# A sparse-attention and mixture-of-experts kernel on one core: keys blocked from PSUM, block sums moved to GpSimd, the last batch in two parts

## The chip, the cores and the metric

The program runs on 1 core of a Trainium2 chip. A core has TensorE (PE in the profile, its weight loads PEld), VectorE (DVE), ScalarE (ACT), GpSimd (POOL) and SyncE (SP, which here only issues DMAs). The metric is the device time of one execution in microseconds.

## The reference

Four batches, eight heads, 768 positions, 64 numbers a head. Each query sees the keys less than 16 positions away, and 24 block keys (the elementwise maximum of 32 keys each) with 24 block values (the mean of 32 values). The result goes through four experts' causal attention; each token uses its best two.

```python
k_sum = k.reshape(B, H, nb, block, D).max(axis=3)     # block = 32, nb = 24
v_sum = v.reshape(B, H, nb, block, D).mean(axis=3)
scores_l = scale * np.matmul(q, k.transpose(0, 1, 3, 2))
mask_l = np.abs(pos[:, None] - pos[None, :]) < window   # window = 16
scores_s = scale * np.einsum('bhsd,bhnd->bhsn', q, k_sum) + np.log(block)
a = softmax(np.concatenate([np.where(mask_l, scores_l, -1e9), scores_s], axis=-1))
x = np.matmul(a, np.concatenate([v, v_sum], axis=2))   # heads side by side: (B, S, 512)
logits = x @ w_gate                                     # best 2 of 4 experts, softmax weights w
for e in range(E):
    q, k, v = x @ wq[e], x @ wk[e], x @ wv[e]
    ye = causal_softmax(scale * (q @ k.transpose(0, 2, 1))) @ v @ wo[e]
    out += (expert e is chosen) * w * ye
```

## The kernel before

The work of each batch has two stages. **Stage 1** goes by pairs of heads (four pairs `c` a batch). The keys and queries of a pair come as 96 rows of 8 positions (`dk`, `dq`, DMAs that GpSimd issues) and are turned on TensorE (`tk`, `tq`: 16 matmuls of 96 columns). The turned keys go from PSUM to a tile `kT` (`ck`), and from there into `kw` (`kw`): 12 overlapping windows of 96 positions for 12 blocks of 64 queries. The block keys come from three halving maxima on VectorE (`km`), two more turned matmuls (L324), a short maximum (`rk`) and a copy of them behind each of the 12 windows (`ksc`). Queries are copied and reordered (`cq`). Then `sc` (mask plus scores, two halves), `ex` (exponentials on ScalarE), `av` (24 matmuls a half, L408), `rc` and `xm` (division), `tx` (turning, L433) and `hi`, `lo` (the result as two 16-bit parts).

The values come straight into `vb` (`dv`): 96 rows for each of 24 windows, so that every window's edge rows are loaded twice. Rows 96 to 119 hold the block sums: `bs` multiplies the windows by a 0-1 matrix `sel` on TensorE (L294), `be` takes them out of PSUM, `ds` copies them to the 12 windows of a head.

**Stage 2** goes by batch: `vp` (values and gate logits), `lg`, `v2`, `ga`, `gx`, `gb`, `gc` (gates); for each of two pairs of experts `pp` (projections, L582), `pc`, six score units `sp` (L606) with exponentials `es` (L614) and GpSimd's causal cut `dm` (L619); `aw` (three pieces, L630); `r2`, `wv` (division and gate), `tw`, `ct` (turning), and for both pairs `op`, `oc`, `od` (output projection, copy, store).

The order is written out by hand: `TABLE` lists each step's number, engine (P, V, A, G, S) and buffer slots, and `emit` issues them so. Each engine runs its own steps in that order, and a step that waits holds up all behind it on its engine. Step names end in batch and pair: `tk12` is pair 2 of batch 1.

## Time and profile before

| | |
|---|---|
| Median of 3 runs | 196.94 us (196.18 to 202.36) |
| Profiled execution, its own time | 197.88 us |
| Its span, first to last instruction | 196.1 us |
| Busy share PE, DVE, ACT, POOL | 83%, 71%, 58%, 41% |
| PE instructions | 3568 matmuls, 3568 weight loads |

Busy shares are means over the span; matmuls are pipelined and their ends are modelled, so PE's share is higher than what its steps need. The chain that ended last names, at each moment, what the end was waiting for; "issue" there is time in which an engine waited for nothing that the profile shows.

### The profile page before, as it was taken

What the parts mean: (1) busy time and instruction counts of PE and PEld (TensorE: products, weight loads), DVE (VectorE), ACT (ScalarE), POOL (GpSimd) and SP (SyncE); (2) the same over time, 40 slices, a digit from 0 to 9 for tenths busy, and PEclk for the clock granted to TensorE, in tenths of its full rate; (3) what the DMA queues carried; (4) which work ended last, traced back from release to release, by engine and by line L of the source; (5) the groups of instructions that cost most, each with busy time, mean ns of one, the idle gap of its engine ahead of it and who ended that gap; (6) DMA issues with size and microseconds to landing.
All of it is one profiled execution on the core that took longest, in us unless ns stands there. A gap on an engine that the chain in (4) does not pass through costs nothing.

```text
span 196.1 us, 7990 instructions
## 1 busy us (share of the span) xinstructions
PE 162.3 (83%) x3568; PEld 127.2 (65%) x3568; DVE 140.0 (71%) x279; ACT 113.1 (58%) x152; POOL 80.3 (41%) x137
## 2 busy tenths in 40 slices
...
GB/s 70 202 208 187 202 173 147 206 192 165 176 228 195 163 76 142 110 199 163 73 3 142 297 190 41 79 3 110 3 214 7 0 5 3 0 3 77 241 128 201
DMA packets 53986, 24.63 MB, mean 126 GB/s; under 512 B 44480, under 2 KB 50624, under 8 KB 53952
## 3 DMA queue, kind: packets, MB, share of 16 engines
...
q14 instruction: 6, 0.05, 0.1%
...
## 4 chain that ended last, share of the span: by engine, by line
PE 66%; DVE 19%; issue 7%; ACT 3%; DMA 3%; DVEq 0%; ACTq 0%; POOLq 0%
PE ps L408 13%; PE ps L582 8%; PE ps L294 7%; PE ps L630 6%; PE ps L433 5%; DVE kw L167 5%; PE ps L671 5%; PE ps L517 4%; PE ps L606 4%; PE ps L384 4%; DVE km L251 3%; PE ps L321 3%; PE ps L391 3%; DMA kn<-in_k_dram 3%; PE ps L362 2%
## 5 line engine op out<-in xcount | busy, mean ns | idle before, releaser
L614 ACT ACTIVATE a<-ps 128x1024 f16<-128x1024 f32 (+1 forms) x48 | 41.9, 918 | 6.5 <-PE ps L606 5.9
L619 POOL TENSOR_SCALAR_AFFINE_SELECT a<-a 128x256 f16<-128x256 f16 x48 | 19.6, 426 | 52.5 <-ACT a L614 52.0
L398 ACT ACTIVATE aT<-ps 120x768 f32<-120x768 f32 x32 | 25.3, 812 | 20.9 <-PE ps L391 18.8
L167 POOL COPY kw<-kT 128x960 f16<-128x960 f16 (+1 forms) x20 | 24.5, 1256 | 25.6 <-ACT kT L165 23.4
L408 PE MATMUL ps<-vb,aT 120*64 120x65 f32 x768 | 28.3, 230 | 5.0 <-issue 3.8
L408 PEld LDWEIGHTS ps<-vb,aT 120*64 120x64 f32 x768 | 25.5, 143 | 7.8 <-issue 5.6
L582 PE MATMUL ps<-hi,wqk 128*128 128x384 f16 x128 | 22.5, 326 | 0.0
L294 PE MATMUL ps<-vb,sel 96*32 96x64 f32 x768 | 18.4, 233 | 4.7 <-issue 4.7
L294 PEld LDWEIGHTS ps<-vb,sel 96*32 96x32 f32 x768 | 16.2, 118 | 6.6 <-issue 6.2
L167 POOL COPY vb<-vs 24x1536 f32<-24x1536 f32 x8 | 12.9, 1611 | 14.5 <-DVE vs L167 12.2
L582 PEld LDWEIGHTS <-wqk 128*128 128x128 f16 x128 | 12.0, 98 | 8.2 <-issue 0.5
L321 PE MATMUL ps<-id,kn 96*64 96x96 f16 x256 | 9.9, 230 | 8.6 <-DMA kn<-in_k_dram 6.6
L423 DVE TENSOR_TENSOR x<-ps,rec 128x768 f32<-128x768 f32 x16 | 15.3, 958 | 0.6
L444 DVE TENSOR_TENSOR lo<-ps,hi 128x768 f16<-128x768 f32 x16 | 14.9, 954 | 0.9 <-ACT hi L165 0.5
L606 PE MATMUL ps<-qk,qk 64*128 64x512 f16 (+3 forms) x128 | 14.7, 307 | 0.7 <-DVE ob L167 0.4
L165 ACT COPY kT<-ps 128x768 f16<-128x768 f16 x8 | 6.4, 801 | 15.2 <-PE ps L324 11.8
L384 PE MATMUL ps<-pi,mt 64*128 64x64 f16 (+1 forms) x128 | 12.7, 271 | 2.8 <-DVE pi L202 1.4
L321 PEld LDWEIGHTS <-kn 96*64 96x64 f16 x256 | 8.3, 128 | 9.8 <-DMA kn<-in_k_dram 6.6
L517 PE MATMUL ps<-wvg,hi 128*128 128x264 f16 x96 | 13.8, 275 | 0.0
L433 PE MATMUL ps<-id,x 128*128 128x128 f32 x96 | 13.3, 278 | 0.1
L671 PE MATMUL ps<-wo,wT 128*128 128x512 f16 x48 | 12.7, 397 | 0.6 <-ACT a L614 0.3
L391 PE MATMUL ps<-qT,kw 64*128 64x64 f16 x384 | 12.5, 201 | 0.0
...
## 6 DMA issues: line engine op xcount, KB each, us to landing
vb<-in_v_dram SPq DMA_DIRECT2D x14, 576.0 KB, 10.2
...
```

The source lines that it names most:

```text
L167: en(e).tensor_copy(dst, src)
L294: nc.tensor.matmul(pbank(sp)[32 * j:32 * j + 32, 0, 0:64], T["sel"][:, 22 - 2 * tt:54 - 2 * tt], T["vb"][vb[b, cs[j // 2]].slot][0:WIN, 12 ...
L321: nc.tensor.transpose(pbank16(kp)[64 * hp:64 * hp + 64, 96 * s:96 * s + 96], src[:, hh + hp, 64 * s:64 * s + 64], T["id16"][0:96, 0:96])
L384: nc.tensor.matmul(s[:, hp, 64 * t0:64 * t1], T["mt"][r, var, :], T["pi"][r, t0:t1, :], start=(i == 0), stop=False, skip_group_check=True)
L398: nc.scalar.activation(T["aT"][aT.slot][0:KR], pbank(sc, 2)[0:KR, :, 0:384], AF.Exp, scale=SCALE)
L408: nc.tensor.matmul(pbank(av, 2)[o:o + 64, u, 65 * (2 * (t // 2) + hp):65 * (2 * (t // 2) + hp) + 65], a[0:KR, hp, 64 * t:64 * t + 64], T[" ...
L433: nc.tensor.transpose(pbank(xp, 2)[:, t // 3, 128 * (t % 3):128 * (t % 3) + 128], T["x32"][x32.slot][:, 128 * t:128 * t + 128], T["id32"])
L517: nc.tensor.matmul(p[:, i, 0:264], hi_(ch)[:, cols], T["wvg"][:, ch, :], start=(ch == 0), stop=False, skip_group_check=True)
L582: nc.tensor.matmul(pbank(pp, 2)[:, u, 0:384], T["wqk"][:, cc, ch, j, :], hi_(ch)[:, 384 * u:384 * u + 384], start=(ch == 0), stop=(ch == N ...
L606: nc.tensor.matmul(pbank(sp, 2)[:, ep, c0:c0 + w], T["qk"][qk[1].slot][r, 128 * tj:128 * tj + 128], T["qk"][qk[0].slot][r, n0:n0 + w], sta ...
L614: nc.scalar.activation(a2v(u), pbank(sp, 2)[:, :, 0:ln], AF.Exp, scale=SCALE / (XS * XS))
L671: nc.tensor.matmul(pbank(op, 2)[:, i, :], T["wT"][wTs[cc].slot][:, 128 * ti:128 * ti + 128], T["wo"][:, cc, :], start=(cc == 0), stop=(cc ...
```

## The change

1. `kw` and `rk` read the turned keys in PSUM themselves. `ck`, `kT`, `km` and the turned maxima are gone; `rk` takes the maximum over all 32 keys. The keys start at PSUM column 2, and two small matmuls fill two columns on either side, so that one copy makes all 12 windows.
2. `dv` loads 64 rows of a window and one column more; `hc` copies the other 32 rows on chip.
3. Block sums stay on TensorE for batch 0 and the first half of batch 1, with both heads of a pair in one matmul of 128 columns. For five groups of four heads (`TREE`), `dvs` loads the values once more, 32 positions a row, and `tr` adds halves on GpSimd; `ds` copies from the result.
4. In the last batch `r2` to `od` run for tiles 0 to 3 and 4 to 5 apart; the last store is two of one tile.
5. 46 matmuls on a tile of zeros stand in front (`f` in the table).
6. `TABLE` is written anew.

```diff
+PE0 = 2
+TREE = {(1, 1), (2, 0), (2, 1), (3, 0), (3, 1)}
...
-SLOTS = dict(qn=3, kn=3, km=3, kT=2, ks=3, kw=3, qT=3, aT=6, x32=2, vb=6, vs=2,
-             rec=2, hi=8, lo=8, v2=2, lgp=2, gt=2, qk=3, a2=2, cmb=2, wav=2,
+SLOTS = dict(qn=3, kn=3, ks=3, kw=3, qT=3, aT=6, x32=2, vb=6, vs=2, vt=1, vu=2,
+             rec=3, hi=8, lo=8, v2=2, lgp=2, gt=2, qk=3, a2=2, cmb=2, wav=2,
...
-116,S,0 27,G,0 28,G,0 29,V,0 30,V, 31,V, 10,G, 76,P,0.0.0 12,V, 5,G,1 77,A, 94,P,1.1.1 99,P,2.0 78,V, 80,V,0
+f,P,7.46 104,S, 2,G,0 0,G, 3,G,0 6,V, 4,G, 53,P,0.0.0 55,V, 36,P,1.1.1 37,A, 56,A, 1,G, 40,P,2.0 38,V, 41,A,
...
-            for w in (256, 128, 64):
-                def mx(e, w=w, i=i):
-                    hs = slice(n * i, n * i + n)
-                    m = T["km"][km[b, g].slot][:, hs, :]
-                    x = T["kn"][kn[b, g].slot][:, hs, :] if w == 256 else m
-                    en(e).tensor_tensor(m[:, :, 0:w], x[:, :, 0:w], x[:, :, w:2 * w], AL.max)
-                ne = w * n
-                R.step(f"km{b}{g}{i}_{w}", {"V": 0.07 + ne * 0.00053},
-                       [kn[b, g]] if w == 256 else [km[b, g]], [km[b, g]], mx)
...
-                          [[D, WIN], [64 * D, t1 - t0], [1, D]])
-            nc.sync.dma_start(out=w[0:WIN, t0:t1, 0:64], in_=src)
-        if edge:
-            R.step(f"zv{b}{c}", {"V": 0.1, "G": 0.14}, [vones], [vb[b, c]], zv)
-        R.step(f"dv{b}{c}", {"S": 0.9 if edge else 0.45}, [vones, vb[b, c]] if edge else [vones],
...
+            src = bass.AP(vh.tensor, vh.offset + (64 * i0 - 16) * D,
+                          [[D, 64], [64 * D, 24 - i0], [1, D]])
+            nc.sync.dma_start(out=w[0:64, i0:24, 0:64], in_=src)
+            t0 = 64 * 24 - 16
+            if last:
+                for h in (0, 16):
+                    nc.sync.dma_start(out=w[h:h + 16, 24:25, 0:64], in_=rows(t0, 16))
+            else:
+                nc.sync.dma_start(out=w[0:32, 24:25, 0:64], in_=rows(t0, 32))
+        R.step(f"dv{b}{c}", {"S": 1.35 if first or last else 0.9}, [], [vb[b, c], vr[b, c]], dv,
+               dma=(64 * 24 + 32) * 0.0215 / 16)
+
+        def edge(e):
+            w = T["vb"][vb[b, c].slot]
+            copy(e, w[64:96, 0:24, 0:64], w[0:32, 1:25, 0:64])
+        R.step(f"hc{b}{c}", {"G": 1.65, "A": 1.45, "V": 0.9}, [vr[b, c]], [vb[b, c]], edge)
...
+        npair = len(cs)
+        ways = 4 // npair
 
         def mm(e):
-            n = 2 * len(cs)
-            for tt in range(NQ):
-                for j in range(n):
-                    nc.tensor.matmul(pbank(sp)[32 * j:32 * j + 32, 0, 0:64],
-                                     T["sel"][:, 22 - 2 * tt:54 - 2 * tt],
-                                     T["vb"][vb[b, cs[j // 2]].slot][0:WIN, 12 * (j % 2) + tt, 0:64],
-                                     start=(tt == 0), stop=(tt == NQ - 1))
-        R.step(f"bs{b}{cs[0]}", {"P": 1.35}, [vb[b, c] for c in cs] + [sel], [sp], mm,
-               mode=3, keep=[t])
+            for tt in range(NQ + 1):
+                for i in range(npair):
+                    j = ways * i + tt % ways
+                    nc.tensor.matmul(
+                        pbank(sp)[32 * j:32 * j + 32, 0, 0:128].rearrange("p (h d) -> p h d", h=2),
+                        T["sel"][:, 24 - 2 * tt:56 - 2 * tt],
+                        T["vb"][vb[b, cs[i]].slot][0:64, tt:tt + 13:12, 0:64],
+                        start=(tt < ways), stop=(tt + ways > NQ))
+        R.step(f"bs{b}{cs[0]}", {"P": 0.03 + 0.054 * npair * 13 * 4 / 4},
...
+            for i in range(npair):
+                dst = T["vs"][t.slot][96:120, i, :]
+                for w in range(ways):
+                    j = ways * i + w
+                    src = pbank(sp)[32 * j:32 * j + NSUM, 0, 0:128]
+                    if w == 0:
+                        copy(e, dst, src)
+                    else:
+                        nc.vector.tensor_tensor(dst, src, dst, AL.add)
+        opts = {"V": 0.25 * 4}
...
             def dsum(e, i=i, c=c):
-                copy(e, T["vb"][vb[b, c].slot][WIN:KR, :, 0:64].rearrange("n (h t) d -> n h t d", h=2),
-                     T["vs"][t.slot][WIN:KR, 2 * i:2 * i + 2, :].unsqueeze(2).to_broadcast(
-                         (NSUM, 2, NQ, 64)))
-            R.step(f"ds{b}{c}", {"G": 1.65, "V": 0.87, "A": 1.4}, [t, vones], [vb[b, c]], dsum)
+                copy(e, T["vb"][vb[b, c].slot][WIN:KR, 0:24, 0:64].rearrange("n (h t) d -> n h t d", h=2),
+                     T["vs"][t.slot][WIN:KR, i, :].rearrange("n (h d) -> n h d", h=2).unsqueeze(
+                         2).to_broadcast((NSUM, 2, NQ, 64)))
+            R.step(f"ds{b}{c}", {"G": 1.55, "V": 0.96, "A": 1.45}, [t], [vb[b, c]], dsum)
...
+    def tree(b, g):
+        t, u = R.buf("vt"), R.buf("vu")
+
+        def load(e):
+            for j in range(4):
+                nc.sync.dma_start(out=T["vt"][t.slot][32 * j:32 * j + NSUM, :],
+                                  in_=v[b, 4 * g + j].rearrange("(n s) d -> n (s d)", s=32))
+        R.step(f"dvs{b}{g}", {"S": 1.8}, [vtz], [t], load, dma=3.0)
+        for i, ws in enumerate(((1024,), (512, 256, 128, 64))):
+            def add(e, ws=ws):
+                x = T["vt"][t.slot]
+                for w in ws:
+                    y = T["vu"][u.slot] if w == 64 else x[:, 0:w]
+                    en(e).tensor_tensor(y[0:120], x[0:120, 0:w], x[0:120, w:2 * w], AL.add)
+            R.step(f"tr{b}{g}{i}", {"G": sum(0.13 + w * 0.00218 for w in ws)}, [t],
+                   [u] if i else [t], add, keep=[t])
+        for c in (2 * g, 2 * g + 1):
+            def dsum(e, c=c):
+                for h in range(2):
+                    j = 32 * (2 * (c % 2) + h)
+                    copy(e, T["vb"][vb[b, c].slot][WIN:KR, 12 * h:12 * h + 12, 0:64],
+                         T["vu"][u.slot][j:j + NSUM, :].unsqueeze(1).to_broadcast((NSUM, NQ, 64)))
+            R.step(f"ds{b}{c}", {"G": 1.75, "V": 0.95, "A": 1.64}, [u], [vb[b, c]], dsum)
...
-        kp, kT, ks, kw = R.buf("ps"), R.buf("kT"), R.buf("ks"), R.buf("kw")
+        kp, ks, kw = R.buf("ps"), R.buf("ks"), R.buf("kw")
+
+        def turn(dst, src):
+            for s in range(8):
+                for hp in range(2):
+                    c0 = PE0 + 96 * s
+                    nc.tensor.transpose(dst[64 * hp:64 * hp + 64, c0:c0 + 96],
+                                        src[:, hh + hp, 64 * s:64 * s + 64], T["id16"][0:96, 0:96])
...
         def tk(e):
             src = T["kn"][kn[b, g].slot]
-            for s in range(8):
-                for hp in range(2):
-                    nc.tensor.transpose(pbank16(kp)[64 * hp:64 * hp + 64, 96 * s:96 * s + 96],
-                                        src[:, hh + hp, 64 * s:64 * s + 64], T["id16"][0:96, 0:96])
+            turn(pbank16(kp), src)
             for hp in range(2):
-                nc.tensor.transpose(pbank16(kp)[64 * hp:64 * hp + 64, 768:864],
-                                    T["km"][km[b, g].slot][:, hh + hp, 0:64], T["id16"][0:96, 0:96])
-        R.step(f"tk{b}{c}", {"P": 0.37}, [kn[b, g], km[b, g], id16], [kp], tk, mode=2, keep=[kT, ks])
-
-        def ck(e):
-            copy(e, T["kT"][kT.slot], pbank16(kp)[:, 0:S])
-        R.step(f"ck{b}{c}", {"V": 0.56, "A": 0.80}, [kp], [kT], ck)
...
+                x = pbank16(kp)[64 * hp:64 * hp + 64, :]
+                nc.tensor.transpose(view(x, 0, [[PE0 + 768, 2], [1, 2]]),
+                                    src[0:4, hh + hp, 0:64], T["id16"][0:4, 0:4])
+        R.step(f"tk{b}{c}", {"P": 0.38}, [kn[b, g], id16], [kp], tk, mode=2, keep=[kw, ks])
+
+        def kwc(e):
+            copy(e, T["kw"][kw.slot][:, :, 0:WIN].rearrange("c t (p s) -> c t p s", s=8),
+                 view(pbank16(kp), 0, [[8, NQ], [1, 12], [96, 8]]))
+        R.step(f"kw{b}{c}", {"V": 1.32, "A": 1.13}, [kp, kwpad], [kw], kwc)
 
...
         def rk(e):
             nc.vector.tensor_reduce(T["ks"][ks.slot],
-                                    pbank16(kp)[:, 768:864].rearrange("c (n p) -> c n p", p=4),
-                                    AX.X, AL.max)
-        R.step(f"rk{b}{c}", {"V": 0.20}, [kp], [ks], rk)
-
-        def kwc(e):
-            w = T["kw"][kw.slot]
-            t = T["kT"][kT.slot]
-
-            def src(off, n, step, m):
-                return bass.AP(t.tensor, t.offset + off,
-                               [list(t.ap[0]), [step, n], [1, m], [96, 8]])
-            copy(e, w[:, 1:NQ - 1, 0:WIN].rearrange("c t (p s) -> c t p s", s=8), src(6, 10, 8, 12))
-            dst = bass.AP(w.tensor, w.offset + 16,
-                          [list(w.ap[0]), [11 * 128 - 16, 2], [8, 10], [1, 8]])
-            copy(e, dst, src(0, 2, 86, 10))
-        R.step(f"kw{b}{c}", {"G": 2.24, "V": 1.20}, [kT, kwpad], [kw], kwc)
+                                    view(pbank16(kp), PE0, [[4, NSUM], [96, 8], [1, 4]]),
+                                    AX.XY, AL.max)
+        R.step(f"rk{b}{c}", {"V": 0.92}, [kp], [ks], rk)
...
+        cuts = [(0, 6)] if b < B - 1 else [(0, 4), (4, 6)]
...
+            for h, (i0, i1) in enumerate(cuts):
...
+                def r2(e, cc=cc, avv=avv, cm=cm, i0=i0, i1=i1):
...
+        outs = [(0, 2), (2, 4), (4, 6)] if b < B - 1 else [(0, 2), (2, 4), (4, 5), (5, 6)]
...
+            R.step(f"op{b}{t2}", {"P": 0.4325 * n}, [wd[0][h], wd[1][h], wo], [op], ops,
+                   keep=[ob] + wTs)
...
     def fill(bank, n):
+        nc.vector.memset(T["zz"], 0.0)
         for _ in range(n):
-            nc.tensor.matmul(T["ps"][:, bank, 0:128], T["id16"], T["id16"], start=True, stop=True)
+            nc.tensor.matmul(T["ps"][:, bank, 0:128], T["zz"], T["zz"], start=True, stop=True)
...
-            if b:
+            if (b, g) in TREE:
+                tree(b, g)
+            elif b:
                 sums(b, [2 * g, 2 * g + 1])
...
-    many("vb", (128, 24, 65), FP32)
-    many("vs", (128, 4, 64), FP32)
+    many("vb", (128, 25, 65), FP32)
+    many("vs", (128, 2, 128), FP32)
+    many("vt", (128, 2048), FP32)
+    many("vu", (128, 64), FP32)
```

What each engine now does, at three places. ScalarE at its start; `kT` are turned keys, `kw` the windows, `ks` block keys, `qT` queries, `aT` exponentials. Before:

```order
L165 ACT_TABLE_LOAD
L165 COPY kT_82<-ps 128x768
L165 COPY qT_91<-ps 128x768
L165 COPY qT_90<-ps 128x768
L398 ACTIVATE aT_94<-ps 120x768
L398 ACTIVATE aT_93<-ps 120x768
L165 COPY qT_92<-ps 128x768
L165 COPY kT_83<-ps 128x768
```

Now:

```order
L166 ACT_TABLE_LOAD
L166 COPY kw_84<-ps 128x12x96
L166 COPY kw_83<-ks_80 128x12x24
L166 COPY qT_86<-ps 128x768
L166 COPY kw_83<-ps 128x12x96
L166 COPY qT_87<-ps 128x768
L429 ACTIVATE aT_89<-ps 120x768
L429 ACTIVATE aT_90<-ps 120x768
```

The copy of turned keys to `kT` is gone, and ScalarE makes the windows itself out of PSUM.

GpSimd in the expert stage of batch 0; `a` are the exponentials that it cuts, `vb` value tiles, `vt` and `vu` the tree's rows. Before:

```order
L167 COPY kw_87<-kT_82 128x10x96
L167 COPY kw_87<-kT_82 128x2x80
L619 AFFINE_SELECT a_136<-a_136 128x2x128 x2
L619 AFFINE_SELECT a_136<-a_136 128x256
L619 AFFINE_SELECT a_136<-a_136 128x2x128 x2
L241 DMA qn_73<-in_q_dram 96x4x512
L167 COPY vb_106<-vs_107 24x24x64
L619 AFFINE_SELECT a_136<-a_136 128x2x128 x3
L619 AFFINE_SELECT a_136<-a_136 128x256
L241 DMA kn_80<-in_k_dram 96x4x512
L619 AFFINE_SELECT a_136<-a_136 128x2x128 x2
```

Now:

```order
L340 TENSOR_TENSOR vt_105<-vt_105 120x1024
L653 AFFINE_SELECT a_136<-a_136 128x2x128
L340 TENSOR_TENSOR vt_105<-vt_105 120x512
L340 TENSOR_TENSOR vt_105<-vt_105 120x256
L340 TENSOR_TENSOR vt_105<-vt_105 120x128
L340 TENSOR_TENSOR vu_107<-vt_105 120x64
L653 AFFINE_SELECT a_136<-a_136 128x256
L653 AFFINE_SELECT a_136<-a_136 128x2x128 x4
L168 COPY vb_100<-vu_107 24x12x64 x2
L168 COPY vb_99<-vb_99 32x24x64
L653 AFFINE_SELECT a_137<-a_137 128x256
```

The windows `kw` have left this queue; the additions of a tree stand between the cuts.

VectorE at the end of the program; `cmb` and `wav` are factors and weighted values, `wT` the turned ones, `ob` output tiles. Before:

```order
L642 RECIPROCAL cmb_138<-ps 128x12
L644 TENSOR_TENSOR cmb_138<-cmb_138,gt_132 128x12
L648 TENSOR_TENSOR wav_140<-ps,cmb_138 128x2x6x64
L642 RECIPROCAL cmb_139<-ps 128x12
L644 TENSOR_TENSOR cmb_139<-cmb_139,gt_132 128x12
L648 TENSOR_TENSOR wav_141<-ps,cmb_139 128x2x6x64
L167 COPY wT_144<-ps 128x768
L167 COPY wT_145<-ps 128x768
L167 COPY ob_146<-ps 128x1024
L167 COPY ob_148<-ps 128x1024
```

Now:

```order
L683 RECIPROCAL cmb_138<-ps 128x2x4
L685 TENSOR_TENSOR cmb_138<-cmb_138,gt_132 128x2x4
L690 TENSOR_TENSOR wav_140<-ps,cmb_138 128x2x4x64
L683 RECIPROCAL cmb_139<-ps 128x2x4
L685 TENSOR_TENSOR cmb_139<-cmb_139,gt_132 128x2x4
L690 TENSOR_TENSOR wav_141<-ps,cmb_139 128x2x4x64
L683 RECIPROCAL cmb_139<-ps 128x2x2
L685 TENSOR_TENSOR cmb_139<-cmb_139,gt_132 128x2x2
L690 TENSOR_TENSOR wav_141<-ps,cmb_139 128x2x2x64
L168 COPY wT_145<-ps 128x256
L168 COPY wT_145<-ps 128x512
L168 COPY ob_148<-ps 128x1024
```

The division of the last expert pair ends with a piece of 2 tiles in place of 6, and one output copy is left here in place of two.

## Rows read from the trace of the kernel before

**Rows 1.** Four stretches: length, busy PE, PEld, DVE, ACT, POOL, PE clock, DMA.

```profile
6.60:43.30 36.70, 30.77 (x804) 27.63 (x805) 28.46 (x60) 19.02 (x30) 18.54 (x32) 1.00 1.19 189
43.30:81.40 38.10, 35.32 (x774) 27.66 (x775) 31.59 (x63) 25.55 (x34) 15.46 (x24) 0.96 1.07 165
81.40:141.00 59.60, 49.65 (x1216) 39.05 (x1215) 44.32 (x85) 34.09 (x47) 30.08 (x36) 0.94 0.60 107
141.00:191.00 50.00, 46.59 (x778) 32.89 (x776) 35.62 (x73) 33.15 (x44) 11.46 (x25) 1.00 0.18 65
```

**Rows 2.** The chain that ended last, shares of the span by engine.

```profile
PE 66%; DVE 19%; issue 7%; ACT 3%; DMA 3%; DVEq 0%; ACTq 0%; POOLq 0%
```

**Rows 3.** The chain in order of time: start, length, what; front and block sums.

```profile
1.36 5.24 DMA kn<-in_k_dram
...
16.26 0.64 PE ps L321 x16
...
31.12 1.50 PE ps L294 x48
...
67.69 1.49 PE ps L294 x96
```

**Rows 4.** The chain: a long copy, and a wait inside block sums.

```profile
52.04 4.35 DVE kw L167 x2
...
111.90 1.15 PE ps L294 x70
113.05 4.31 issue
117.36 1.01 PE ps L294 x26
```

**Rows 5.** The chain: TensorE steps at full clock.

```profile
38.60 1.42 PE ps L408 x48
...
50.86 0.34 PE ps L321 x16
...
86.62 0.47 PE ps L517 x4
...
138.25 1.31 PE ps L433 x12
...
152.16 2.60 PE ps L582 x16
```

**Rows 6.** Instructions grouped by line and shape: count, busy us, mean ns, idle before.

```profile
L614 ACT ACTIVATE a<-ps 128x1024 f16<-128x1024 f32 x40 | 39.4, 1025 | 3.8 <-PE ps L606 3.4
...
L398 ACT ACTIVATE aT<-ps 120x768 f32<-120x768 f32 x32 | 25.3, 812 | 20.9 <-PE ps L391 18.8 <-DVE vs L167 1.9
...
L165 ACT COPY qT<-ps 128x768 f16<-128x768 f16 x11 | 8.7, 804 | 6.5 <-PE ps L362 6.5
...
L167 DVE COPY qT<-ps 128x768 f16<-128x768 f16 x5 | 4.7, 948 | 0.5 <-PE ps L362 0.5
```

**Rows 7.** The same view, two copies on GpSimd.

```profile
L167 POOL COPY kw<-kT 128x960 f16<-128x960 f16 x10 | 19.4, 1942 | 25.6 <-ACT kT L165 23.4 <-DVE kT L167 2.2
...
L167 POOL COPY vb<-vs 24x1536 f32<-24x1536 f32 x8 | 12.9, 1611 | 14.5 <-DVE vs L167 12.2 <-PE ps L391 2.1
```

**Rows 8.** Instructions in order of time: block-key copies on VectorE, a GpSimd copy.

```profile
12.70 2.48 POOL L167 COPY kw<-kT 128x960 f16<-128x960 f16 x2 [0.84 <-DVE kT L167]
...
13.01 1.85 DVE L167 COPY kw<-ks 128x288 f16<-128x288 f16 x1
...
19.74 0.24 DVE L167 COPY kw<-ks 128x288 f16<-128x288 f16 x1
```

**Rows 9.** DMA issues: count, KB each, median us from issue to landing.

```profile
vb<-in_v_dram SPq DMA_DIRECT2D x14, 576.0 KB, 10.2
```

**Rows 10.** The chain: the end of the program.

```profile
182.82 1.29 PE ps L630 x42
...
189.78 1.23 DVE ob L167
```

297 lines of the change are left out of this document (151 added, 146 removed).

## The prediction

> **What bounds the kernel now.** I read the chain of waits first, then busy time by stretch, then single steps. The chain is 66% TensorE, 19% VectorE and 7% issue [rows 2]: TensorE sets the pace, but much of it is waiting. I cut the run where the projections (`pp`) of batches 0, 1 and 2 begin: 6.6 to 43.3 us (stage A), to 81.4 (B), to 141.0 (C), and to the last engine instruction at 191.0 (D). In these 36.7, 38.1, 59.6 and 50.0 us [rows 1] PE shows 31 to 50 us busy, but a matmul's row holds its latency too, so I count PE by steps, from back-to-back rows at full clock [rows 5]: a projection step `pp` (8 matmuls of 384 columns) 1.30 us, 0.423 ns a column; by that rate a score step `sc` 0.33 to 0.35, the 12 `sp` of a batch 2.3 to 2.4, an output step `op` 0.87; a value step `vp` 2 x 0.47 and small matmuls, 1.1; `av` 0.71; `tx` 0.66; a turn `tk` or `tq` 0.34; `aw` 0.43 a piece, from 1.29 for three [rows 10]; `tw` 0.34. A block-sum step is 1.5 either way, 48 matmuls with two side by side or 96 with four [rows 3].
>
> Stage B before: 4 `pp` 5.2, 3 `vp` 3.3, `sp` 2.4, 5 turns 1.8, 2 `bs` 3.0, 4 `sc` 1.4, 8 `av` 5.7, 4 `tx` 2.6, 6 `aw` 2.6, 2 `tw` 0.7, 2 `op` 1.7: 30.3 us. The same count gives 41.6 for C and 42.6 for D. So PE works 30.3 of 38.1 (0.79), 41.6 of 59.6 (0.70), 42.6 of 50.0 (0.85). In A, VectorE is the fullest, 28.46 of 36.7 (0.776) [rows 1]. The rest is waits between engines. Three kinds are plain. TensorE runs at half clock in the front: 16 turns take 0.64 us there and 0.34 later [rows 3, 5], 1.2 against 2.4 GHz. VectorE's copies from SBUF to SBUF stand still while GpSimd works: a copy of block keys takes 1.85 us beside a GpSimd copy and 0.24 elsewhere [rows 8], and the windows `kw` once held the chain for 4.35 us [rows 4]. And TensorE stops for 4.31 us inside one block-sum step, after 70 of 96 matmuls and with no step's wait in between [rows 4]: it seems to have had no instructions.
>
> **The change, part by part.** *Block sums.* 768 matmuls (10 steps, 15.0 us) become 156 of 128 columns: twice the columns, so 2 x 1.49/96 = 31 ns each, 4.8 us. TensorE saves 10.2 us. Nothing else fills that time on PE.
>
> *Instructions of PE.* 3568 matmuls become 3568 - 612 + 46 = 3002, 16% fewer, and the block sums, which use up instructions fastest (16 ns a matmul), are mostly gone. I count the 4.31 us stop as gone and leave the other issue pieces. The Trainium skill, "Runtime: NRT & Kernel Launch", Instruction fetch mechanics, says that fetching is mostly hidden, since instructions issue more slowly than they are loaded; by that the stop has another cause and stays, and stage C below would be 3.5 us longer. The row inside the step speaks against it.
>
> *Keys.* `ck`, `km` and GpSimd's `kw` leave. `kw` now reads 1152 elements in PSUM: ScalarE takes 0.80 us for 768 and 1.03 for 1024 [rows 6], so 1.13; below 0.80 is excluded, and above I allow 1.4. Queries are read with the same step today, at 0.80. `rk` reads 768 in place of 96 elements, 0.95 as VectorE's query copy [rows 6]. So VectorE loses its long SBUF work and gains 16 x 0.7 us in PSUM.
>
> *Values.* `hc` copies 32 rows of 1536 elements, which is GpSimd's 1.6 us of `ds` [rows 7]; 13 run there. A tree adds 1984 elements: between 1.05 ns (that copy) and 2.0 ns an element (the strided `kw` copy, 1942 ns for 960) [rows 7], 2.1 to 4.0 us; two inputs make me take 4.0. In C GpSimd then has 3 trees 12, 15 `dm` 6.2, `hc` and `ds` 11, DMA issues and the rest 4: 33 us, a little below the others.
>
> *Front.* The zeros run within the 5.2 us that the first keys take [rows 3]; 46 at 57 to 114 ns (128 columns, full or half clock) need 2.6 to 5.2 us and cost nothing; without that cover they would cost up to that. They may leave the clock at full; A is bound elsewhere, so I credit nothing. Value loads no longer wait for GpSimd's clearing and now run beside the first keys: 0 to 2 us later keys, 0.5 taken.
>
> *End.* Before: last `aw` ends at 184.1, last copy at 191.0 [rows 10], 6.9 us. Now two small VectorE operations 0.4, a third of `wv` 0.4, 2 turns 0.2, copy 0.3, six output tiles 2.6 and a copy of one tile 0.6, with hand-overs some 5.3: 1.6 saved. The last store is half as large: 5.1 us behind the last copy become 4.6.
>
> **The sum.** Work of the fullest engine in each stage of the new order, over the share that was reached there. A: ScalarE, 7 `kw` 7.9, 8 `cq` 6.4, 11 `ex` 8.9, 3 `hi` 2.4, 3 `ksc` 1.3, `ds` 1.5: 28.4 (VectorE 27.9, PE 20.9); over 0.776, 36.6. B: PE 25.0 (30.3 less 3 `aw`, two turns, one `bs`, one `tw`, two `op`, and one `sc` more), VectorE 24.6, ScalarE 24.0; over 0.79, 31.6. C: PE 36.0, VectorE 36.2, ScalarE 35.4; the share without the stop is 41.6 of 55.3, 0.75, so 48.0. D: PE 44.9 (more of batch 3's `av` and `tx` fall here), ScalarE 39.9, VectorE 38.6; over 0.85, 52.8, less the end's 1.6. With 7.1 in front and 4.6 behind: 7.1 + 36.6 + 31.6 + 48.0 + 51.2 + 4.6 = 179.1. The profiled execution was 197.88 us with a span of 196.1, so 1.8 lie around it; the median is 0.9 lower. **Forecast: 180 us.** With 0.85 in every stage the four are 134.3/0.85 = 158.0, and the time 169; with 0.74, 181.5, and the time 192.
>
> **Rivals.** *(a) Three full engines.* ScalarE goes from 112 [rows 1] to 129 us, VectorE from 140 to some 128, PE falls to 127. If what PE gives back is eaten by waits for these two, only the block sums' 10.2 us go: 187. For it: the shares above were reached with one full engine; against it: part of VectorE's 140 were waits for GpSimd.
>
> *(b) VectorE stands still beside GpSimd.* GpSimd goes from 80 to some 100 us, and 13 SBUF copies remain on VectorE (`ksc` 5, `ds` 6, `hc` 2). If each is stretched by the 1.6 us of [rows 8], VectorE has 21 us more, some 17 of it on the path: 197 us, no change. Against it: 26 such copies (`kw`, `ksc`, `ds`) and 27 `km` stood there before. The Trainium skill, "SBUF — State Buffer", Who interferes with whom, has the rule: whichever of GpSimd and a VectorE copy in a two-port mode starts first holds the shared port pair for its whole instruction. By that rule PSUM reads are free of it, and the rows agree as far as the block-key copy goes.
>
> *(c) The trees come late; slower.* There is one tile `vt`. A tree's load waits for the last one's additions, and SyncE holds all later value loads and stores behind it, GpSimd all later `dm`, for which `aw` waits. A cycle is a landing, 10.2 us as a value load's [rows 9], and 4 us of adding; four of them fit into the 80 us of B and C. From 20 us a cycle on they don't: at 26, PE waits 6 us four times, 204 us.
>
> *(d) Still faster.* All shares at 0.85 or more, below 169 us.
>
> **How the numbers follow.** Forecast with its spread, 169 to 185: 0.56. (a), 185 to 193: 0.24. (b), 193 to 201: 0.08. (c), above 201: 0.07. (d): 0.05. Two per cent, about what a measurement of this kernel can tell from no change, is 193 to 201. The range 169 to 193 leaves out 0.20. Faster 0.85, same 0.08, slower 0.07.
>
> **What would show it.** The projections of batches 0, 1 and 2 begin near 44, 75 and 123 us; PE shows some 3000 matmuls and L294's successor about 5 us; no issue piece above 2 us; windows from PSUM near 1.13 us on ScalarE; a tree near 4 us; VectorE busy near 128 us. Wrong would be: a wait of `dm` or `ds` for a tree's load, VectorE copies of block keys above 1 us all over, the first keys landing after 9 us, or stage A longer than 37 us because ScalarE's queue, which now holds seven window copies, holds back the exponentials.

## The result and the profile after

The changed kernel takes 187.2 us (median of four runs, 184.9 to 187.9) where the kernel before, run beside it, takes 198.4. The ratio is 0.948, with an interval from 0.932 to 0.965; run once more in E1 it is 0.941 (0.931 to 0.951). The forecast of 180 us named the direction, and its range holds the time, but the gain is 11 us and not 17. Single runs of one kernel lie up to 8 us apart here (183.9 to 192.2 in E1), so small differences are read from the intervals and from stretches of the trace, not from single times. The ratios compare only the fast runs of both kernels, those within some 1.5% of the fastest of their kernel, so a median that holds slower runs can lie higher than its ratio suggests.

The page of the changed kernel (busy time by engine; queue, packets, MB and share; the chain by engine):

```profile
span 186.2 us, 6923 instructions
...
PE 158.9 (85%) x3002; PEld 122.4 (66%) x3002; DVE 131.9 (71%) x254; ACT 120.8 (65%) x155; POOL 100.1 (54%) x150
...
q8 instruction: 23, 0.38, 1.0%
...
PE 48%; DVE 22%; DMA 9%; issue 7%; POOL 6%; ACT 5%; POOLq 0%; DVEq 0%; ACTq 0%
```

TensorE has its 3002 matmuls and GpSimd its 100 us, as worked out; ScalarE has 121 us and not 129, VectorE 132 and not 128. Yet "issue", time in which TensorE waits for nothing that the profile shows, is 7% as before [rows 2]. The queue q8 carries instructions: 0.38 MB in 23 packets are 16 KB each; and 0.44 MB (0.06 more come by another queue) for 6923 instructions are 64 bytes each. So a packet holds 256 instructions, for TensorE 128 weight loads with their matmuls. The kernel before had 28 such packets for 7990 instructions.

The four stretches of the prediction, in the changed kernel (windows; columns as in [rows 1]):

```profile
6.10:45.10 39.00, 31.65 (x770) 27.12 (x770) 27.51 (x65) 23.99 (x30) 18.23 (x28) 0.82 1.24 183
45.10:78.50 33.40, 30.03 (x561) 23.72 (x560) 26.11 (x46) 23.85 (x30) 21.67 (x26) 0.95 0.95 137
78.50:126.90 48.40, 41.85 (x855) 31.69 (x855) 38.62 (x63) 33.48 (x45) 37.90 (x51) 1.00 0.87 157
126.90:181.40 54.50, 50.28 (x777) 35.02 (x774) 39.38 (x79) 38.21 (x51) 17.69 (x32) 1.00 0.28 82
```

| us | before | forecast | after | after less forecast |
|---|---|---|---|---|
| up to the first keys | 6.6 | 7.1 | 6.1 | -1.0 |
| A | 36.7 | 36.6 | 39.0 | +2.4 |
| B | 38.1 | 31.6 | 33.4 | +1.8 |
| C | 59.6 | 48.0 | 48.4 | +0.4 |
| D | 50.0 | 51.2 | 54.5 | +3.3 |
| behind | 5.1 | 4.6 | 4.8 | +0.2 |
| span | 196.1 | 179.1 | 186.2 | +7.1 |

The gain comes from B and C; A is longer than before. The front, in the timeline of TensorE (start, length, line, what, idle time before and its end):

```profile
6.08 0.85 PE L360 MATMUL ps<-id,kn 96*64 96x96 f16 x16
...
7.00 0.56 PE L360 MATMUL ps<-id,kn 96*64 96x96 f16 x16
...
11.13 1.49 PE L360 MATMUL ps<-id,qn 96*64 96x96 f16 x32 [3.45 <-DMA qn<-in_q_dram]
```

The first keys are turned at 6.08 us, half a microsecond earlier than before and not half a microsecond later. The queries are late instead: TensorE stands for 3.45 us, and behind that it works at half rate again (32 turns in 1.49 us; 16 took 0.56 just before, and 32 take 0.87 at 111.38). The costs of single steps (groups: busy, mean ns):

```profile
L340 POOL TENSOR_TENSOR vt<-vt 120x1024 f32<-120x1024 f32 (+3 forms) x20 | 25.0, 1248 | 5.5 <-DMA vt<-in_v_dram 4.3
...
L381 DVE TENSOR_REDUCE ks<-ps 128x24 f16<-128x768 f16 x16 | 14.9, 952 | 10.1 <-PE ps L371 5.9
...
L168 POOL COPY vb<-vb 32x1536 f32<-32x1536 f32 x13 | 18.9, 1461 | 2.8 <-DMA vb<-in_v_dram 2.1
...
L166 ACT COPY kw<-ps 128x1152 f16<-128x1152 f16 x10 | 11.2, 1121 | 12.9 <-PE ps L371 7.2
```

The window copy (1.12 us for 1.13), the maxima (0.95) and the edge copy (1.46 for 1.6) are as priced. The row of the trees holds four of a tree's five additions; with the last, narrow one (1.6 us for all five) a tree is 26.6/5 = 5.3 us, above the bounds of 2.1 to 4.0. The block sums left on TensorE show 7.1 us busy, where about 5 were expected.

Last, the stops, the pieces of the chain called "issue" (start, length, what):

```profile
30.23 1.64 issue
...
56.05 2.09 issue
58.14 0.28 PE ps L640
58.42 4.51 PE ps L439 x96
...
105.59 2.34 POOL vt L340
...
120.12 1.16 issue
```

The stop of 4.31 us inside a block-sum step [rows 4] is gone, but the text had counted on no stop above 2 us, and there is one of 2.09, with 96 matmuls of `av` behind it at 47 ns each, where they take 33 at full rate (72 in 2.41 us at 72.08); the granted clock is 0.50 in the first 2 us of them. At 105.59 the chain runs over GpSimd's tree; E12 shows what that is.

### The profile page after: what moved, and what is told of

Same layout as the page of the kernel before. It is cut to its first block, busy times and chain, and to the rows that moved or that the text cites. A ratio compares the mean times of both kernels' runs of the same rounds, so it can differ in the third digit from the quotient of the medians.

```text
span 186.2 us, 6923 instructions
## 1 busy us (share of the span) xinstructions
PE 158.9 (85%) x3002; PEld 122.4 (66%) x3002; DVE 131.9 (71%) x254; ACT 120.8 (65%) x155; POOL 100.1 (54%) x150
## 4 chain that ended last, share of the span: by engine, by line
PE 48%; DVE 22%; DMA 9%; issue 7%; POOL 6%; ACT 5%; POOLq 0%; DVEq 0%; ACTq 0%
PE ps L439 10%; PE ps L616 7%; DMA vb<-in_v_dram 5%; PE ps L464 5%; PE ps L360 5%; DMA qn<-in_q_dram 4%; PE ps L548 4%; PE ps L718 3%; PE ps L640 3%; POOL vt L340 3%; DVE ks L381 2%; DVE wav L690 2%; PE ps L415 2%; PE ps L297 2%; PE ps L664 2%
## 5 line engine op out<-in xcount | busy, mean ns | idle before, releaser
L653 POOL TENSOR_SCALAR_AFFINE_SELECT a<-a 128x256 f16<-128x256 f16 x48 | 18.6, 406 | 42.1 <-ACT a L648 29.3
L340 POOL TENSOR_TENSOR vt<-vt 120x1024 f32<-120x1024 f32 (+3 forms) x20 | 25.0, 1248 | 5.5 <-DMA vt<-in_v_dram 4.3
L381 DVE TENSOR_REDUCE ks<-ps 128x24 f16<-128x768 f16 x16 | 14.9, 952 | 10.1 <-PE ps L371 5.9
L168 POOL COPY vb<-vb 32x1536 f32<-32x1536 f32 x13 | 18.9, 1461 | 2.8 <-DMA vb<-in_v_dram 2.1
L166 ACT COPY kw<-ps 128x1152 f16<-128x1152 f16 x10 | 11.2, 1121 | 12.9 <-PE ps L371 7.2
L415 PE MATMUL ps<-pi,mt 64*128 64x320 f16 (+1 forms) x128 | 11.8, 259 | 3.5 <-POOL vt L340 2.6
L360 PE MATMUL ps<-id,qn 96*64 96x96 f16 x256 | 9.0, 226 | 4.3 <-DMA qn<-in_q_dram 3.4
L664 PE MATMUL ps<-v,a 128*128 128x65 f16 x336 | 12.0, 193 | 0.6 <-ACT wT L166 0.6
L664 PEld LDWEIGHTS <-a 128*128 128x128 f16 x336 | 11.2, 97 | 2.0 <-issue 1.4
L166 ACT COPY qT<-ps 128x768 f16<-128x768 f16 x11 | 8.6, 805 | 5.9 <-PE ps L360 5.9
```

The costliest lines, as they stand in the source:

```text
L166: nc.scalar.copy(dst, src)
L168: en(e).tensor_copy(dst, src)
L340: en(e).tensor_tensor(y[0:120], x[0:120, 0:w], x[0:120, w:2 * w], AL.add)
L381: nc.vector.tensor_reduce(T["ks"][ks.slot], view(pbank16(kp), PE0, [[4, NSUM], [96, 8], [1, 4]]), AX.XY, AL.max)
L664: nc.tensor.matmul(pbank(av, 2)[:, ep, 65 * ti:65 * ti + 65], a2v(u)[:, ep, o:o + 128], T["v2"][v2.slot][:, tj, 2 * cc + ep, :], start=(tj ...
```

## The experiments

All were run beside the kernel before, and the column of the ratio is against it (for E12 too few runs could be compared). `pp` is where the projections of batches 0, 1 and 2 begin in the profiled run, and D+ the time from the last of these to the end of the span.

| | median (lowest to highest), us | ratio (95% interval) | profiled span | pp 0, 1, 2 | D+ |
|---|---|---|---|---|---|
| after | 187.2 (184.9-187.9) | 0.948 (0.932-0.965) | 186.2 | 45.1, 78.4, 126.8 | 59.5 |
| E1 after again | 186.7 (183.9-192.2) | 0.941 (0.931-0.951) | 185.0 | 47.1, 76.5, 125.6 | 59.5 |
| E2 no zeros | 191.3 (187.8-193.5) | 0.957 (0.948-0.967) | 190.8 | 51.9, 82.3, 130.1 | 60.7 |
| E3 values held | 189.9 (183.8-191.6) | 0.936 (0.924-0.947) | 189.7 | 45.9, 79.8, 130.2 | 59.5 |
| E4 held, zeros | 188.5 (184.4-191.9) | 0.940 (0.930-0.949) | 188.5 | 47.1, 79.1, 127.9 | 60.6 |
| E5 short keys | 191.5 (187.6-192.7) | 0.956 (0.947-0.965) | 190.1 | 49.4, 81.5, 130.6 | 59.5 |
| E6 light trees | 194.9 (193.6-196.7) | 0.990 (0.983-0.996) | 192.4 | 47.2, 82.7, 132.6 | 59.8 |
| E7 sums on TensorE | 234.9 (234.1-236.2) | 1.194 (1.188-1.200) | 232.4 | 45.5, 80.7, 143.4 | 89.0 |
| E8 one tail | 189.8 (184.9-191.9) | 0.944 (0.935-0.954) | 190.2 | 46.8, 80.0, 130.3 | 59.8 |
| E9 thin trees | 193.1 (189.6-197.8) | 0.973 (0.952-0.994) | 187.9 | 47.4, 80.2, 128.4 | 59.5 |
| E10 third of sums | 190.8 (188.4-194.3) | 0.964 (0.946-0.982) | 187.3 | 42.8, 80.6, 132.2 | 55.1 |
| E11 warm front | 191.0 (187.6-193.7) | 0.958 (0.929-0.988) | 185.9 | 49.5, 78.6, 126.4 | 59.5 |
| E12 spread moved | 190.4 (186.0-191.7) | none | 189.0 | 46.6, 78.6, 129.5 | 59.5 |

**E1.** The changed kernel, unaltered.

> The changed kernel unaltered, as the mark for the runs beside it. It stood at 187.2 us (184.9 to 187.9). If its gain is the block sums' matmuls and little else, the four stretches repeat within 1 us: 39.0, 33.4, 48.4 and 54.5 us. If chance transfers made the first profile late, the front (first score matmul at 12.87 us) and the stops of TensorE without a named wait (2.09 us at 56.05, 1.64 us at 30.23) move to other places or sizes.

The gain repeats, but not the stretches: A is 2 us longer, B 4 us shorter (29.4), C 0.7 longer, D the same within 0.1. The stops of 1.64 and 2.09 us are both gone, while the wait for the queries stays (3.43 us). So the second reading holds for the stops, which come and go from run to run, and not for the front.

**E2.** Without the zeros.

```
-f,P,7.46 104,S, 2,G,0 ...
+104,S, 2,G,0 ...
```

> The changed kernel without the 46 matmuls on zeros. The prediction credited them with nothing: then the time stays within 1 us of the changed kernel, and the first 16 turns take 0.85 us again, as they do with the zeros. Rival: they lift the clock for what follows; then the second 16 turns, 0.56 us with the zeros, take 0.64 or more, and the time rises by some 0.3 us up to, if the clock in the whole first stretch depends on them, 3 us.

The ratio is 0.957 for E1's 0.941, some 3 us, and the two intervals still overlap (0.948 to 0.951), so that the zeros are worth anything is likely and not shown. If they are, it is not the front: without the zeros the first queries are turned at 10.75 (E1: 11.00) and the first `av` starts at 21.71 (21.95). The profiled run loses its time later, in stops of 3.16 us at 31.95, 1.66 at 48.78 and 2.35 at 113.0. "Credited with nothing" is in doubt, and the rival's reason was wrong.

**E3.** The first value load held.

```
+ if (b, g, i, name) == (0, 0, 0, "q"):
+     nc.gpsimd.memset(T["vb"][0][0:64, 0:2, 0:64], 0.0)
```

> The changed kernel, but the first value load waits for a small GpSimd memset placed behind the first issue of queries, as GpSimd's clearing held it before. Theory F (front): the first queries were late because value loads of 368 KB and more ran beside them: TensorE's wait of 3.45 us shrinks to 1 to 2 us, the first score matmul comes at 10.5 to 11.5 us in place of 12.87, and the time falls by 1 to 2 us. Rival: the delay is not on the path, since the half clock and VectorE set the first stretch; then the first scores move but the second stretch begins within 0.5 us of 45.1 and the time stays. Third: values now land later than they are used, and the time rises by 1 us or more.

The wait for queries shrinks from 3.4 to 2.2 us and the first scores come at 11.42: theory F is right on the cause. On the time the rival is nearer: the intervals of E1 and E3 overlap for the most part.

**E4.** The same, with zeros in the gap.

```
- ... 36,P,1.1.1 37,A, ...
+ ... 36,P,1.1.1 f,P,7.40 37,A, ...
```

> As the run with the first value load held, and 40 more matmuls on zeros between the first keys' turns and the first queries' turns, where TensorE has nothing to do. If the granted clock fell to 1.2 GHz (0.50 from 16 to 24 us) because TensorE stood still for 3.45 us there, the clock of 8 to 24 us rises to 0.9 or more, turns and scores there take half as long, and the time falls by 2 to 4 us against the run with the load held alone. Rival: the clock falls later anyway, in the many short waits of the first stretch, or the first stretch is held by VectorE and ScalarE: then the clock rises for a few us at most and the time stays within 1 us.

The rate stays up until 14.7 us (32 query turns in 0.87 us at 9.16, where E3 takes 1.49) and falls behind the next gaps; the granted clock is 0.50 from 16 to 24 us again. The time stays, as the rival had it.

**E5.** Short key maxima.

```
- view(pbank16(kp), PE0, [[4, NSUM], [96, 8], [1, 4]])
+ view(pbank16(kp), PE0, [[4, NSUM], [96, 1], [1, 4]])
```

> The changed kernel, but the key maxima (rk) read one of eight sub-rows, 96 elements of PSUM in place of 768, so that the block keys are not the real ones. VectorE has 16 x some 0.75 us = 12 us less, and the chain turn, window copy, maxima, spread is 0.75 us shorter in each pair. Theory K (rival a of the prediction: what TensorE gave back is eaten by waits for VectorE and ScalarE, here because window copy and maxima read one PSUM bank and run one after the other): 4 us or more off the 187, most of it in the first three stretches (39.0, 33.4, 48.4). Rival: TensorE's own work and its stops hold the stretches; then 2 us or less.

VectorE falls from 131.9 to 121.4 us busy, and no time comes off; the ratio is if anything higher. Its stops (counted below) add up to 9.2 us and E1's to 3.5, but without them too the two spans are nearly alike, 180.9 and 181.5 us. Theory K falls: what TensorE gave back is not eaten by waits for VectorE's maxima.

**E6.** Light trees.

```
  for w in ws:
+     if 64 < w < 1024:
+         continue
+     if w == 1024:
+         w = 16
```

> The changed kernel, but of the trees' 1984 additions GpSimd makes 80 (16 and 64 columns), so that the block sums of those groups are not the real ones; loads, order and waits stay. GpSimd has 5 x some 4.6 us = 23 us less. If the trees are off the path (the prediction's sum, which has TensorE or VectorE as the fullest), under 1 us comes off 187. If GpSimd holds the path where a tree stands in front of the diagonal masks, the spreads or the block-key copies (2.56 us of TensorE's wait at 110.62), 2 to 5 us, in the second and third stretch, and VectorE's spread of sums (1369 ns) gets shorter.

GpSimd falls from 100 to 76 us, and the kernel is slower by 5%. VectorE's spread of sums does get shorter, so GpSimd does hold it up elsewhere (the line of the changed kernel has 1369 ns):

```profile
L168 DVE COPY vb<-vs 24x1536 f32<-24x1536 f32 x3 | 2.9, 964 | 0.1
```

but the kernel as a whole gains nothing by it. There is a stop inside a score step, here in the chain of E6:

```profile
115.53 0.06 PE ps L426 x3
115.59 4.05 issue
119.64 0.44 PE ps L426 x9
```

With another of 2.02 us that is 2.5 us more in stops than E1 has, of the 7.3 us by which E6's span is longer; the rest is not explained.

**E7.** The trees' sums on TensorE.

```
-TREE = {(1, 1), (2, 0), (2, 1), (3, 0), (3, 1)}
+TREE = set()
```

(with the steps `bs`, `be`, `ds` of these groups in the table ahead of and behind their `hc`).

> One part undone: the five trees are replaced by block sums on TensorE in the new form (three pair steps of 52 matmuls and four single steps of 26), evicted by VectorE, all placed just before the edge copy of their value tile. TensorE has some 7 to 8 us more, VectorE 6 to 7 us more, GpSimd 25 us less. By the prediction's sum, in which TensorE's work over a share of 0.75 to 0.85 sets the second to fourth stretch, the time rises by 8 to 10 us, to about 196. If GpSimd's trees cost the path nearly as much as they give back, it stays within 2 us of 187.

48 us more is far beyond either. The sums of VectorE (waits view of E7: us in total, times, longest) show where some of it goes:

```profile
POOL vb L168 <- DVE vs L315: 67.7, 7, 16.5
...
PE ps L439 <- POOL vb L168: 13.0, 4, 4.5
```

Behind a sum step VectorE's four short operations, GpSimd's spread and the edge copy that now stands behind it follow one another before `av` can start: TensorE waits 13.0 us for GpSimd there and 6.2 more for VectorE, and works at a mean granted clock of 0.84, where the changed kernel has 0.95. How the 48 us divide is not shown. This prices the place in the order, not the work of the sums, so it is no answer to the question. It does show what the trees buy: their additions need no place in TensorE's queue.

**E8.** One tail.

```
-cuts = [(0, 6)] if b < B - 1 else [(0, 4), (4, 6)]
+cuts = [(0, 6)]
```

(and three stores of two tiles).

> One part undone: the last batch's attention output is weighted, turned and stored as in the other batches, in one piece each and three stores of two tiles. The prediction credited the two parts with 1.6 us ahead of the last copy and 0.5 us behind it: then some 2 us more, 189, and from the last value matmul of the experts to the last engine instruction 7 us in place of 5.7. Rival: the extra small steps cost as much as they hide, and the time stays within 0.7 us.

D+ is 59.8 for 59.5: the split is worth 0.3 us, not 2.1. Behind the last `aw` 7.3 us pass (178.3 to 185.6) where the split has 5.7, the expected saving; but the split makes TensorE wait for the first part's `wav` and `wT` ahead of the last `aw`. Timeline of TensorE at the end of the changed kernel:

```profile
173.84 0.40 PE L700 MATMUL ps<-id,wav 128*128 128x128 f16 x4 [0.36 <-DVE wav L690]
174.89 0.83 PE L664 MATMUL ps<-v,a 128*128 128x65 f16 x22 [0.65 <-ACT wT L166]
```

**E9.** Thin trees: the same instructions, two columns wide.

```
+ n = w if w == 64 else 2
...
- ... x[0:120, 0:w], x[0:120, w:2 * w], ...
+ ... x[0:120, 0:n], x[0:120, w:w + n], ...
```

> The changed kernel with all 25 tree additions in place, but the four large ones of each tree only 2 columns wide, so that the block sums of those groups are not the real ones. The run with light trees (15 of these instructions left out) rose to 194.9 us with a stop of TensorE of 4.05 us at 115.6 and one of 2.02 us at 57.1, each beside an instruction packet. Theory S (stops): TensorE's stops for instructions, and the half rate behind them, decide more than the trees; their places hang on where the packets fall. With the same instructions as the changed kernel but GpSimd 23 us emptier, the stop of 4 us goes or moves, and the time is 184 to 188. Theory G: less work on GpSimd itself makes the kernel slower, by the order of the transfers that it lets start earlier; then 193 to 196 again. By a plain reading (trees on the path for the 2.0 to 2.6 us that TensorE waits for one at about 109), 184.

The median of 193 stands with theory G, the profiled run of 189.6 nearer to theory S: the stop of 4.05 us is gone, and there are others of 1.77 us at 65.2 and 2.13 at 113.8. So the two are not told apart. What both runs tell is that an emptier GpSimd does not make the kernel faster; why it is slower stays open.

**E10.** The kernel before, with a third of its block-sum matmuls.

```
- for tt in range(NQ):
+ for tt in (0, 4, 8, NQ - 1):
```

> The kernel before with one part of the change alone, in price: its block-sum steps issue 4 of every 12 matmuls (256 in place of 768), so that the sums are not the real ones; TensorE has 10.0 us less of them at full rate, as the prediction's 10.2 us. If TensorE sets the pace, 8 to 10 us come off its 197 to 198, to 188 or 189, and with the stop inside a sum step (4.31 us) gone too, 184 to 186. If the time is handed to waits for VectorE and GpSimd (whose key maxima and window copies stay), 3 us or less. The change as a whole gave 11 us.

8 us come off, in the lower part of the first expectation, but not as the prediction's sum has it. A and B give 0.5 and 0.2 us, though six of the ten steps stand there. All the rest is C, 59.6 to 51.6 us: its three steps are worth 3 us of work, and its stops shrink from 6.8 us (0.89, 4.31, 1.63) to 2.76.

**E11.** A warm front: zeros in six gaps, values held.

```
+ f,P,7.40 (ahead of tq00), 7.10 (sc001), 7.14 (bs00), 7.15 (tk03), 7.9 (tk02), 7.42 (tq02)
```

> The changed kernel with the first value load held behind the queries' issue, and 130 more matmuls on zeros in TensorE's waits of the front: 40 ahead of the first queries' turns, 10 ahead of the first scores, 14 ahead of the first block sums, 15 and 9 ahead of the next key turns, 42 ahead of the next query turns. In the runs so far TensorE did 16 turns in 0.85 us until 22 to 33 us, and its row was full from 24 to 32 us with the granted clock at 0.50. Theory C: these gaps let the clock fall, and the half rate is on the path; filled, the clock stays at 1.00 from 6 to 33 us, batch 0's projections begin at 40 to 42 us in place of 45 to 47, and the time falls to 181 to 184. Rival: VectorE and ScalarE hold the first stretch; the clock stays up, batch 0's projections begin within 1 us of 45, and the time stays at 185 to 190. Third: the clock falls all the same.

Windows of E11:

```profile
8.00:16.00 8.00, 6.66 (x157) 5.68 (x155) 3.79 (x28) 5.08 (x7) 1.21 (x4) 1.00 1.21 181
16.00:24.00 8.00, 7.33 (x191) 6.55 (x192) 6.44 (x8) 2.85 (x4) 7.47 (x10) 1.00 1.08 148
24.00:32.00 8.00, 5.02 (x108) 3.88 (x108) 3.49 (x10) 3.46 (x5) 0.47 (x1) 0.72 1.30 190
```

and of E1:

```profile
8.00:16.00 8.00, 4.76 (x92) 3.86 (x94) 3.54 (x26) 5.00 (x7) 5.78 (x5) 0.63 1.35 194
16.00:24.00 8.00, 6.63 (x137) 6.01 (x140) 5.20 (x8) 4.23 (x6) 2.88 (x7) 0.50 1.34 184
24.00:32.00 8.00, 8.00 (x140) 6.56 (x134) 4.46 (x11) 3.11 (x4) 1.85 (x1) 0.50 1.25 202
```

The clock is held at 1.00 to 24 us, and batch 0's projections still begin at 49.5. A stop of 2.98 us at 25.85 takes the clock down after all. Before that ScalarE had stood 6.14 us ahead of its third window copy (at 20.57), for VectorE's maxima, and these stood behind a spread of sums that took 2.38 us. So the half clock alone is not what makes A long. (E11 holds the value load too, and its first block sums wait 1.06 us for values.)

**E12.** One spread of block keys moved from VectorE to ScalarE.

```
- ... 565,A, 454,A, 567,V, 434,P,0.5 ...
+ ... 565,A, 454,A, 567,A, 434,P,0.5 ...
```

> The changed kernel with one copy moved: the spread of the block keys of batch 3's first pair of heads (96 us into the program's third stretch, 0.29 us on VectorE at 109.06 in the first profile, 0.30 at 107.18 in the second) is done by ScalarE, which stands idle there for 2.4 us. In both profiles TensorE's next score matmul waits 2.56 and 1.98 us and is released when an addition of GpSimd's tree ends. Theory P (the prediction's rival b): VectorE's copy from SBUF to SBUF is not done before GpSimd's addition ends; on ScalarE it takes 0.43 us, TensorE's wait there shrinks to 0.8 us or less, and the third stretch to 46.5 us. Rival: the score matmul waits for something of the tree itself; then the wait stays at 2 us or more. In the whole time theory P gives 1.2 to 2.2 us, 184.5 to 186, unless stops for instructions fall in other places, which moved the time by up to 8 us in the runs before.

(The copy stands some 30 us into the third stretch; the 96 is a slip.) Timeline of E1 at this place, TensorE:

```profile
105.85 0.34 PE L415 MATMUL ps<-pi,mt 64*128 64x64 f16 x3
108.17 0.31 PE L415 MATMUL ps<-pi,mt 64*128 64x320 f16 x1 [1.98 <-POOL vt L340]
```

and of E12, ScalarE and TensorE:

```profile
108.29 0.43 ACT L166 COPY kw<-ks 128x288 f16<-128x288 f16 x1
...
107.98 0.34 PE L415 MATMUL ps<-pi,mt 64*128 64x64 f16 x3
110.96 0.44 PE L415 MATMUL ps<-pi,mt 64*128 64x320 f16 x1 [2.64 <-issue]
```

The copy is done at 108.7, and TensorE still stands for 2.64 us, after the same third matmul of the score step, now with no engine named. The tree was not what it waited for, and nor was VectorE's copy: both the expectation's theory and its rival fall. In E2, without the 46 zeros, the same matmul runs without a wait while a tree is at work, and TensorE stops 46 matmuls later, after the same count of 1875:

```profile
111.65 0.34 PE L415 MATMUL ps<-pi,mt 64*128 64x64 f16 x4
...
115.36 0.53 PE L360 MATMUL ps<-id,qn 96*64 96x96 f16 x15 [2.35 <-issue]
```

The stop goes with the count and not with the step. It is a stop for instructions, and the profile had put it down to the tree whose addition ended next to it.

**The stops, counted.** For each stop I counted by windows from 0 the matmuls up to it. Of the changed kernel (41 counts of this kind stand in the table):

```profile
0.00:30.60 30.60, 23.77 (x475) 20.84 (x476) 16.38 (x52) 14.58 (x18) 16.42 (x34) 0.78 1.17 167
0.00:56.40 56.40, 46.68 (x985) 39.18 (x985) 38.45 (x86) 33.29 (x41) 31.45 (x50) 0.88 1.16 170
0.00:108.50 108.50, 93.85 (x1875) 75.06 (x1875) 80.01 (x158) 72.11 (x90) 70.30 (x105) 0.92 1.03 158
0.00:120.50 120.50, 102.94 (x2130) 82.90 (x2130) 88.07 (x170) 79.60 (x100) 77.73 (x112) 0.93 1.02 162
```

| | stops in us (matmuls before them) |
|---|---|
| before | 1.76 (350), 0.89 (2135), 4.31 (2262), 1.63 (2518) |
| after | 1.64 (475), 2.09 (985), 2.56 (1875), 1.16 (2130) |
| E1 | 1.98 (1875), 1.56 (2130) |
| E2 | 3.16 (475), 1.66 (729), 2.35 (1875) |
| E3 | 2.83 (1875) |
| E4 | 1.32 (729), 2.37 (1112), 1.47 (1875), 1.49 (2130) |
| E5 | 1.00 (348), 2.69 (475), 1.84 (857), 2.37 (1875), 1.33 (2130) |
| E6, E7 | 2.02 (985), 4.05 (2003); 1.93 (475), 2.49 (2133) |
| E8, E9 | 2.19 (985), 2.51 (1875), 1.70 (2130); 0.91 (857), 1.77 (1112), 0.84 (1875), 2.13 (2003) |
| E10 | 1.28 (350), 1.42 (1112), 2.76 (1878) |
| E11, E12 | 2.98 (476), 2.65 (2003); 0.80 (985), 2.64 (1875) |

The 1875 of the changed kernel, E1, E3, E5 and E8 stands in the profile as a wait for GpSimd's tree, that of E9 as one for its copy. The counts recur in kernels that do different work there, with zeros and without, and they are multiples of 127 to 128 apart (475, 729, 857, 985, 1112; 1875, 2003, 2130): a packet's 256 instructions, with a few that are no matmul. And an instruction packet moves beside each. The queue's line of the changed kernel, once from 55.0 us to the end and once from 55.5 (packets, MB, share):

```profile
q8 instruction: 17, 0.28, 0.4%
...
q8 instruction: 16, 0.26, 0.4%
```

One packet starts in that half microsecond, 0.5 to 1 us before the stop of 2.09. Of the kernel before, from 114.0 and from 114.5:

```profile
q8 instruction: 12, 0.20, 0.3%
...
q8 instruction: 11, 0.18, 0.3%
```

That one starts some 1 to 1.5 us into the stop of 4.31, which ends 2.9 to 3.4 us later. Since one packet goes with every 128 matmuls, a packet nearby is little by itself; its end tells more. In the packet records of all fourteen traces, each stop of 0.8 us or more for which no engine is named ends 1.3 to 1.7 us after a packet of this queue, whether it lasted 0.8 or 4.3 us, and those put down to GpSimd at 1875 end 1.2 to 1.6 us after one; TensorE's other waits of that length end anywhere between 0 and 11 us after one. So these stops are waits for instructions: shown by the place and by the packet's end. That the packets are late because the 16 engines of the DMA are full of data is argued only: the DMA share is 1.24, 0.95 and 0.87 in A to C, and 0.28 in D, where TensorE has no such stop of more than 1 us in any run. It fits that, taken in order, one packet to a border, the six packets of D in the changed kernel start within 12 matmuls of theirs, and 16 of the 17 in A to C 18 to 127 matmuls late.

The stops alone do not explain how far the versions lie apart. Without them the spans of those with the changed kernel's work are 179 to 187 us, and the three longest (E3, E6, E12) have the lowest mean granted clock, 0.90.

## Why the prediction was right, and where it was off

**Bound.** TensorE sets the pace in B to D, and the gain is in B and C: right in kind. E10 corrects the reading of the sum, though. The 10.2 us of block sums were counted as work that leaves the path. Taking 10 us of them out of the kernel before gave 0.7 us in A and B together and 8 in C, of which some 4 are stops that got shorter. By the ratios (0.964 for 0.941 to 0.948) that leaves 3 to 5 us for the rest of the change, and no run takes the windows out of PSUM or the shorter value loads back by themselves, so what each of them gave is open.

**Instructions.** "I count the 4.31 us stop as gone and leave the other issue pieces": this step failed. The pieces named in the table add up to 8.6 us before and 7.4 after. Fewer matmuls mean fewer packets, 23 for 28, but each border of 128 matmuls can be the place of a stop, and new ones came at 475, 985 and 1875. B shows what that can cost: 33.4 us with a stop of 2.09 and the half rate behind it, 29.4 without (E1), 2.2 less than forecast; but A is 2.0 longer there, and the two together are 70.4 for 72.4. C came out at 48.4 for 48.0 with 3.7 us of stops in it, where the share of 0.75 had left in the 2.5 of 0.89 and 1.63; other waits in that share did not come, and so close a hit is luck in part. The text set the 4.31 us row against the Trainium skill ("Runtime: NRT & Kernel Launch", Instruction fetch mechanics). By the Trainium skill a block is 256 instructions, and the trace agrees, by 16 KB packets and by the spacing of the counts. The Trainium skill also has the cost of a border as mostly hidden, and there the traces differ: 0.8 to 4.3 us at one to five borders of every run.

**Keys and values.** The single prices were right, but for the block sums left on TensorE (7.1 us for 5) and the tree: 5.3 us, outside the bounds, since additions with two inputs take 2.7 ns an element over the whole tree, and the bound was 2.0 from a copy with one. It cost nothing that shows: E6 and E9 take the trees' work away, and no time comes off.

**Front.** Keys came 0.5 us earlier, queries 3.45 us late: the right cause (value loads beside them, E3), on the wrong transfer. "The zeros cost nothing" was right and "credited with nothing" is in doubt: some 3 us by the ratios, between intervals that overlap (E2). They don't warm the front. What they do change is where the borders fall in the work, 46 matmuls earlier; that this is the whole of their worth is not shown.

**A.** Forecast at 36.6 with ScalarE fullest; 39.0 to 46.5 in the versions. The condition named for this, ScalarE's queue, is not what the rows show: ScalarE has 24.0 us busy there, 4.4 less than counted. TensorE at half rate until 23 to 33 us, the late queries and stops of 1.6 to 3.2 us stand there together, and taking one of them (E3, E4, E11) brought out another. Which of them is worth what stays open.

**D.** The share of 0.85 was too high by itself: with one tail it is 55.2 us (E8), for the forecast 52.8. And the split's 1.6 us are 0.6 up to the last instruction: 1.5 saved behind the last `aw`, 1.0 paid ahead of it; the smaller last store saves nothing (4.8 us behind the last instruction, 4.6 with one tail). D+ is 59.5 to 59.8 in nine of the eleven versions that have its work, so this term is firm: 3.3 of the 7.1 us.

**Rivals.** The time lies in the band of (a), 185 to 193, but, as far as VectorE goes, not by its mechanism: E5 takes 10 us from VectorE for nothing. ScalarE, its other engine, no run made lighter. (b) is real and small. VectorE's copies are stretched beside GpSimd (the spread of sums 1369 ns against 964 in E6), and E12 caught one that TensorE waits for, as E3 did at the same count (1.28 us) (timeline of E12, VectorE, GpSimd, TensorE):

```profile
118.50 3.19 DVE L168 COPY vb<-vu 24x768 f32<-24x768 f32 x2
...
118.68 5.47 POOL L340 TENSOR_TENSOR vt<-vt 120x1024 f32<-120x1024 f32 x4 [4.18 <-DMA vt<-in_v_dram]
...
121.75 1.27 PE L439 MATMUL ps<-vb,aT 120*64 120x65 f32 x36 [1.21 <-DVE vb L168]
```

In the changed kernel the same two copies take 1.14 us, since they are over before the tree begins. The second copy ends at 121.69, just behind the tree's first addition (2.60 us, to 121.28 in E12's chain). That is as the Trainium skill ("SBUF — State Buffer", Who interferes with whom) has it: the one that starts first holds the shared ports for its whole instruction. This wait comes after 2068 matmuls, at no border. The price of 1.6 us a copy lies between the 1.2 (2.17 us for 0.97, the changed kernel) and 2.0 (E12) seen; the thirteen copies were wrong: in the changed kernel one of them meets a tree. (c): the trees wait 4.3 us for their loads in all, and no wait of `dm` for one shows in the page. (d) did not come: no run was under 183.7 us.

No version beats the changed kernel beyond its interval. Holding the value load (E3, 0.936) has the lowest ratio.
